# Three groups' sums in one pair of PSUM banks, and the variance floor made once per twelve tiles

## The chip, the cores and the metric

The kernel runs on one core of a Trainium2 chip. The metric is the device time of one execution in microseconds. Five engines work side by side, each through its own instructions in order: PE (matmuls; its weight loads have rows of their own, PEld), DVE, ACT, POOL and SP, which here only issues DMAs. They wait for each other through semaphores.

## The reference

Two stages follow each other: attention through 32 inducing points (each batch's tokens are pooled into 32 vectors, then each token attends to these), and a feed-forward layer whose activation is `h * softmax(h)` with a layer norm over the 1,024 hidden values. Cut to what matters (`e` is the exponential, `c` the token's row):

```python
h = mab(I, x)                 # per batch: 32 pooled vectors from 12608 tokens
y = mab(x, h)                 # each token attends to the 32 vectors
hid = y @ w_in                # 128 -> 1024
e = exp(hid - max(hid))
solu = hid * e / (sum(e) + 1e-9)
ln = (solu - mean(solu)) / sqrt(var(solu) + 1e-6) * g_ln
out = ln @ w_out              # 1024 -> 128
```

There are 4 batches of 12,608 tokens and 128 features, all in float32.

## The kernel before, in words

A tile is 128 tokens; a batch has 99 tiles (the last one half full), the four batches 396. Tiles go in groups of four (the last group of a batch has three), 25 groups a batch. Three groups make a set (`FG = 3`): eight full sets and one set of a single group per batch, 36 sets in all.

A batch's first pass (`p1`: loading x, transposing it, pooling) runs among the previous batch's tiles, except for batch 0, whose first pass runs alone at the start. `p2` makes the attention weights of twelve tiles at a time. Then each tile goes through `main`, `soft` and `products`:

- PE makes the 1,024 hidden values of the tile (L958) in a PSUM buffer of two banks; DVE multiplies by the token's factor and takes the negated maximum (L996);
- ACT takes the exponential and sums it into S, one column per tile (L1006);
- POOL multiplies by the hidden values (L1010), which takes 2.37 us and is the longest step of a tile;
- ACT squares the product and sums it into Q (L1021); DVE transposes it in 32x32 blocks into the group's `vt` (L1034);
- when a group's four tiles are in `vt`, its product with the weights `wc` starts (`products`, L1079). It runs in two streams, w = 0 and 1, of 32 steps each. A stream owns two of the four 32-row groups of the PE array and two PSUM banks, `op0` or `op1`. A step of one stream, which I call a beat, is two matmuls. Where both streams are open their beats go side by side; the hidden values (L958) and the transposes (L551) also use only half of the array and are paired with a beat of one stream. Where nothing is paired with it, a beat has the array to itself.

The matmul has 129 columns: 128 outputs and the sum over the hidden values, from a column of ones. When a stream's 32 beats are done, `evacuate` copies its two banks (2 x 129 columns) to the set's buffer `raw` (L1101), on DVE or ACT, whichever the planner finds first. The lock `OP[w]` has one buffer: the stream's next group starts when the copy is done.

The layer norm is finished once per set, since the division by the sum of exponentials cancels against the variance up to the floor 1e-6, which becomes (1e-3 S)^2. `floor` (per group) makes this on POOL in two small instructions (L1051, L1052), writes it beside Q, and deals Q and the floor through DRAM into the token order of the products (one DMA out, L1055, and one in per tile, L1063). `finish` (per set) makes the variance, its inverse root and a Newton step on POOL and ACT (L1122 to L1141), and then scales the set's outputs group by group, either as four ACT instructions (L1156) or as one POOL instruction (L1152). `stored` writes them out.

The order of every engine is settled at build time by `Planner`. Each step is an `Op` with an engine, an estimated cost, the steps it follows, a priority (the tile's number plus an offset), and perhaps an alternative engine (`alt`). The planner always takes the engine that could start something first, and of what is ready there the step with the lowest priority. So a changed cost or a step on another engine can move all steps behind it, on every engine.

```python
pick = min(
    (o for o in self.ops if o[0].eng == eng and o[1] <= limit),
    key=lambda o: (o[2][1] if o[0].prio is None else o[0].prio, o[3]),
)
```

Of the kernel before, what the change touches and what calls it, by code (L numbers as in the profile page):

```python
# [8 lines left out]
F32 = mybir.dt.float32  # L9
# [237 lines left out]
def set_attention_then_solu_kernel(ctx: ExitStack, tc: tile.TileContext, x, inducing, w_in, w_out, g_ln, out):  # L247
# [38 lines left out]
    def small(i, **widths):  # L286
# [20 lines left out]
    OP = [Lock(), Lock()]  # L307
    HN, EU = Lock(hn_b[:1]), Lock()
# [9 lines left out]
        dict(qe=buf([P, GS, 2], f"qe{i}"), S=buf([P, GS], f"st{i}"), dd=dd_pool.tile([P * 2 * GS], F32, name=f"dd{i}")) for i in range(4)  # L318
# [3 lines left out]
        dict(dl=buf([P, 4 * FG, 2], f"dl{i}"), **dict(zip(("part", "v", "y", "root", "z"), split(buf([P, 5, 4 * FG], f"fin{i}")))))  # L322
# [588 lines left out]
    fin = {(b, f): dict(buf=Event(), out=[], left=2 * min(FG, NG - f * FG)) for b in range(NB) for f in range(-(-NG // FG))}  # L911
# [74 lines left out]
    def soft(t, hp, d):  # L986
# [14 lines left out]
        if not A["left"]:  # L1001
# [4 lines left out]
            "ACT", 1133, lambda: nc.scalar.activation(e, hn, AF.Exp, bias=nm, scale=-1.0, accum_out=G["S"][:, s : s + 1]), d, rel, srel,  # L1006
# [39 lines left out]
    def floor(b, j):  # L1046
        G = grp[(b, j)]
        n = ff_groups[j][1]
        ep = G["qe"][:, :n, 1]
        gt, gs = nc.gpsimd.tensor_tensor, nc.gpsimd.tensor_scalar  # L1050
        d = yield Op("POOL", 165, lambda: gs(out=ep, in0=G["S"][:, :n], scalar1=1e-3, scalar2=1e-12, op0=ALU.mult, op1=ALU.add), G["squared"])  # L1051
        d = yield Op("POOL", 125, lambda: gt(out=ep, in0=ep, in1=ep, op=ALU.mult), d)  # L1052
        flat = G["dd"][: P * 2 * n].rearrange("(p f) -> p f", f=2 * n)
        ds = yield dma(
            P * 8 * n, lambda: nc.sync.dma_start(flat, G["qe"][:, :n, :].rearrange("p s v -> p (s v)")), d, G["squared"], prio=-30, issue=600  # L1055
        )
        F = fin[(b, j // FG)]
        rel = yield F["buf"]
        dl = F["dl"][:, j % FG * 4 : j % FG * 4 + 4, :]
        laid = G["dd"][: P * 2 * n].rearrange("(a t s v) -> s t a v", a=4, t=M, v=2)  # L1060
        dealt = []
        for s in range(n):
            d = yield dma(P * 8, lambda: nc.sync.dma_start(dl[s * M : (s + 1) * M], laid[s]), ds, rel, prio=-30, issue=600)  # L1063
            dealt.append(d)
        plan.set(G["floor"], *dealt)
        give(ST, G["stb"], *dealt)

    def products(b, j, t, w):
# [4 lines left out]
        op, rel = yield OP[w]  # L1073
# [3 lines left out]
        def emit(a, k):  # L1077
            q = slice(a * M, (a + 1) * M)
            nc.tensor.matmul(op[:rows, a - 2 * w, : C + 1], lhsT=vt[q, k, :], rhs=wc[q, k, :], start=(k == 0), stop=(k == JB - 1))  # L1079
# [13 lines left out]
    def evacuate(b, j, w, op, dop, prio):  # L1093
# [3 lines left out]
        i0 = j % FG * 4 + 2 * w  # L1097
        rel = yield F["buf"]

        def copied(eng):  # L1100
            return lambda: eng(F["raw"][:rows, i0 : i0 + 2, :], op[:rows, :, : C + 1])  # L1101

        d = yield Op("DVE", 340, copied(nc.vector.tensor_copy), dop, rel, prio=prio, alt=Op("ACT", 265, copied(nc.scalar.copy), dop, rel, prio=prio))
# [6 lines left out]
    def finish(b, f):  # L1110
# [8 lines left out]
        part, v, y, root, z = (F[k][:rows, :w] for k in ("part", "v", "y", "root", "z"))  # L1119
        Q, ep = (F["dl"][:rows, :w, i] for i in range(2))  # L1120
        gt, gs = nc.gpsimd.tensor_tensor, nc.gpsimd.tensor_scalar
        d = yield Op("ACT", 110, lambda: nc.scalar.activation(part, F["raw"][:rows, :w, C], AF.Square, scale=1.0 / FF), F["out"])  # L1122
# [153 lines left out]
```

## Time and profile before

| | us |
|---|---|
| median of 3 runs (1237.88 to 1242.12) | 1241.6 |
| the profiled execution, its own time | 1239.79 |
| its span | 1238.0 |
| mean granted clock of PE | 0.984 |

The profile is of one execution. A row of a group of instructions has the line, engine, operation, output and inputs, shapes and count; behind the bar the busy time, the mean length of one in ns, and the idle time ahead of them with what ended it. A row of the waits has who waited for whom, the total in us, how often, and the longest. A timeline row begins with start and length in us. Matmul counts are twice those of the program, since a float32 matmul shows as two.

### The profile page before, as it was taken

What the parts mean: (1) busy time and instruction counts of PE and PEld (TensorE: products, weight loads), DVE (VectorE), ACT (ScalarE), POOL (GpSimd) and SP (SyncE); (2) the same over time, 40 slices, a digit from 0 to 9 for tenths busy, and PEclk for the clock granted to TensorE, in tenths of its full rate; (3) what the DMA queues carried; (4) which work ended last, traced back from release to release, by engine and by line L of the source; (5) the groups of instructions that cost most, each with busy time, mean ns of one, the idle gap of its engine ahead of it and who ended that gap; (6) DMA issues with size and microseconds to landing.
All of it is one profiled execution on the core that took longest, in us unless ns stands there. A gap on an engine that the chain in (4) does not pass through costs nothing. (4 is left out here: it accounts for less than half of the span.)

```text
span 1238.0 us, 79230 instructions
## 1 busy us (share of the span) xinstructions
PE 1199.9 (97%) x35686; PEld 1113.8 (90%) x35686; DVE 1126.6 (91%) x1822; ACT 1126.7 (91%) x2408; POOL 1100.6 (89%) x984
## 2 busy tenths in 40 slices
PE   9889999999999999999999999999999999999995
PEld 6688899999899999999999998989999999999995
DVE  5669999999998999989999999999999999999982
ACT  5569999999899999999999999999989999999993
POOL 2569889889998999989999999998989999999994
PEclk9869999999999999999999999999999999999998
DMA  9462334322233333233133224432122222211111
GB/s 355 177 155 64 120 110 131 107 68 79 56 89 114 113 99 113 85 107 91 47 93 120 62 73 133 124 122 70 43 81 58 58 56 56 56 48 38 30 31 42
DMA packets 134867, 113.69 MB, mean 92 GB/s; under 512 B 79072, under 2 KB 87168, under 8 KB 134400
## 3 DMA queue, kind: packets, MB, share of 16 engines
q1 hardware_dynamic: 134528, 108.63, 29.6%
q8 instruction: 279, 4.57, 1.5%
q14 instruction: 60, 0.49, 0.1%
HBM read 54.30 MB, written 52.18 MB: 86 GB/s over the span
## 5 line engine op out<-in xcount | busy, mean ns | idle before, releaser
L1079 PE MATMUL op<-wc,vt 32*128 32x129 f32 x25600 | 1020.0, 274 | 8.2 <-DVE vt L1034 1.9
L1079 PEld LDWEIGHTS op<-wc,vt 32*128 32x128 f32 x25600 | 976.5, 185 | 47.3 <-issue 32.1
L1010 POOL TENSOR_TENSOR eu<-spare,eu 128x1024 f32<-128x1024 f32 x192 | 454.0, 2372 | 33.0 <-ACT eu L1006 30.1
L958 PE MATMUL h<-hs,aT 32*128 32x128 f32 x6336 | 431.3, 277 | 7.1 <-DVE spare L996 3.1
L1034 DVE STREAM_TRANSPOSE vt<-eu 128x1024 f32<-128x1024 f32 x330 | 404.0, 1231 | 6.9 <-POOL eu L1010 6.9
L958 PEld LDWEIGHTS h<-hs,aT 32*128 32x128 f32 x6336 | 388.5, 189 | 21.8 <-DVE spare L996 6.8
L1021 ACT ACTIVATE sq<-eu 128x1024 bf16<-128x1024 f32 x330 | 346.9, 1051 | 34.2 <-POOL eu L1010 29.8
L1010 POOL TENSOR_TENSOR eu<-hn,eu 128x1024 f32<-128x1024 f32 x138 | 326.8, 2374 | 21.6 <-ACT eu L1006 19.5
L996 DVE TENSOR_SCALAR_CACHE_REDUCE spare<-h,rn 128x1024 f32<-128x1024 f32 x228 | 286.5, 1263 | 22.3 <-PE h L958 10.9
L996 DVE TENSOR_SCALAR_CACHE_REDUCE hn<-h,rn 128x1024 f32<-128x1024 f32 x168 | 211.0, 1263 | 13.9 <-PE h L958 5.6
L1006 ACT ACTIVATE eu<-spare,nm 128x1024 f32<-128x1024 f32 x192 | 218.9, 1141 | 4.2 <-DVE spare L996 3.6
L1006 ACT ACTIVATE eu<-hn,nm 128x1024 f32<-128x1024 f32 x138 | 157.3, 1141 | 0.1
L1156 ACT ACTIVATE os<-spare,fin 128x128 f32<-128x128 f32 (+1 forms) x276 | 86.4, 389 | 2.9 <-DMA out_dram<-os 1.8
L1010 POOL TENSOR_TENSOR spare<-spare 128x1024 f32<-128x1024 f32 x36 | 85.4, 2373 | 0.8 <-ACT spare L1006 0.7
L1034 DVE STREAM_TRANSPOSE vt<-spare 128x1024 f32<-128x1024 f32 x66 | 81.3, 1232 | 2.3 <-POOL spare L1010 2.0
L1021 ACT ACTIVATE sq<-spare 128x1024 bf16<-128x1024 f32 x66 | 69.4, 1052 | 5.8 <-POOL spare L1010 4.8
L1010 POOL TENSOR_TENSOR spare<-hn,spare 128x1024 f32<-128x1024 f32 x30 | 71.2, 2373 | 2.9 <-ACT spare L1006 2.8
L1101 DVE COPY spare<-op 128x258 f32<-128x258 f32 (+1 forms) x123 | 50.8, 417 | 20.0 <-PE op L1079 18.4
L1021 ACT ACTIVATION_READ_ACCUMULATOR sq<-eu 128x1 f32 x330 | 62.7, 190 | 0.0
L551 PE MATMUL h<-ident,xn 32*128 32x32 f32 x1188 | 45.5, 220 | 0.4 <-issue 0.4
L551 PEld LDWEIGHTS h<-ident,xn 32*128 32x128 f32 x1188 | 44.1, 137 | 1.2 <-ACT spare L1101 0.6
L608 ACT COPY xT<-h 128x768 f32<-128x768 f32 (+2 forms) x54 | 39.6, 733 | 2.9 <-PE h L551 2.8
(166 smaller groups left out, 1026.0 us busy)
## 6 DMA issues: line engine op xcount, KB each, us to landing
xT<-xd SPq DMA_DIRECT2D x96, 256.0 KB, 3.3
out_dram<-os SPq DMA_DIRECT2D x96, 256.0 KB, 2.3
xn<-in_x_dram SPq DMA_DIRECT2D x73, 256.0 KB, 3.2
xd<-xT SPq DMA_DIRECT2D x72, 256.0 KB, 2.5
dl<-dd SPq DMA_DIRECT2D x396, 1.0 KB, 2.7
xd<-vt SPq DMA_DIRECT2D x7, 768.0 KB, 11.0
spare<-in_x_dram SPq DMA_DIRECT2D x5, 768.0 KB, 12.8
wc<-hn SPq DMA_DIRECT2D x16, 128.0 KB, 2.7
```

Of the source, the lines that this page charges most:

```text
L551: nc.tensor.transpose(out=tr[:h, at : at + M], in_=block[rows, :h], identity=ident[rows, rows])
L608: nc.scalar.copy(in_rows(xT[:, :n, :], c0), from_rows(tr, n))
L958: nc.tensor.matmul(hp[:, cols], lhsT=aT[rows, i // 2, :], rhs=hs[rows, cols], start=True, stop=True)
L996: lambda: nc.vector.tensor_scalar(out=hn, in0=hp, scalar1=rn, scalar2=None, op0=ALU.mult, op1=ALU.min, accum_out=nm),
L1006: "ACT", 1133, lambda: nc.scalar.activation(e, hn, AF.Exp, bias=nm, scale=-1.0, accum_out=G["S"][:, s : s + 1]), d, rel, srel,
L1010: d = yield Op("POOL", 2330, lambda: nc.gpsimd.tensor_tensor(out=e, in0=hn, in1=e, op=ALU.mult), de, prio=t + PR_MU)
L1021: "ACT", 1040, lambda: nc.scalar.activation(sq, e, AF.Square, scale=1.0 / 32.0, accum_out=G["qe"][:, s, 0:1]), d,
L1034: lambda: nc.vector.transpose(out=G["vtb"][:, : n * FF].rearrange("p (j s t) -> p j s t", j=M, s=n)[:, :, s, :], in_=e.rearrange("p (a f) ...
L1079: nc.tensor.matmul(op[:rows, a - 2 * w, : C + 1], lhsT=vt[q, k, :], rhs=wc[q, k, :], start=(k == 0), stop=(k == JB - 1))
L1101: return lambda: eng(F["raw"][:rows, i0 : i0 + 2, :], op[:rows, :, : C + 1])
L1156: nc.scalar.activation(os[:rows, q, :], raw[:, q, :], AF.Copy, scale=y[:, i0 + q : i0 + q + 1])
```

## The change

The sums of a set's three groups go side by side into the same two banks of a stream: group i of the set writes columns 129 i to 129 (i + 1). A new lock `TURN[w]` lets a stream take the groups in order; it is given on when a group's last beat is planned, without a copy between. Only the set's first group takes `OP[w]`, and only its last starts `evacuate`, which copies all columns at once (2 x 387 of them, or 2 x 129 for the single group at a batch's end). The planner's costs for the copy become 90 + 269 k on DVE and 90 + 215 k on ACT for k groups.

The floor's two POOL instructions go. ACT sums the exponentials straight into the buffer that is dealt, beside Q, so S and Q are dealt; `finish` makes the floor for the whole set with one ACT Square, with scale 1e-3 and bias 1e-12, after the dealt data have landed.

```diff
+    TURN = [Lock([None]), Lock([None])]
...
-        dict(qe=buf([P, GS, 2], f"qe{i}"), S=buf([P, GS], f"st{i}"), dd=...) for i in range(4)
+        dict(qe=buf([P, GS, 2], f"qe{i}"), dd=...) for i in range(4)
...
-            "ACT", 1133, lambda: nc.scalar.activation(e, hn, AF.Exp, ..., accum_out=G["S"][:, s : s + 1]), d, rel, srel,
+            "ACT", 1133, lambda: nc.scalar.activation(e, hn, AF.Exp, ..., accum_out=G["qe"][:, s, 1:2]), d, rel, srel,
...
     def floor(b, j):
-        ep = G["qe"][:, :n, 1]
-        d = yield Op("POOL", 165, lambda: gs(out=ep, in0=G["S"][:, :n], scalar1=1e-3, scalar2=1e-12, ...), G["squared"])
-        d = yield Op("POOL", 125, lambda: gt(out=ep, in0=ep, in1=ep, op=ALU.mult), d)
...
-            ..., lambda: nc.sync.dma_start(flat, G["qe"]...), d, G["squared"], prio=-30, issue=600
+            ..., lambda: nc.sync.dma_start(flat, G["qe"]...), G["squared"], prio=-30, issue=600
...
     def products(b, j, t, w):
-        op, rel = yield OP[w]
+        F, i = fin[(b, j // FG)], j % FG
+        yield TURN[w].at(b * NG + j)
+        rel = ()
+        if not i:
+            F["op"][w], rel = yield OP[w]
+        op = F["op"][w]
...
-            nc.tensor.matmul(op[:rows, a - 2 * w, : C + 1], ...)
+            nc.tensor.matmul(op[:rows, a - 2 * w, i * (C + 1) : (i + 1) * (C + 1)], ...)
...
-            spawn(evacuate(b, j, w, op, d, t + PR_EV), t + PR_EV)
+            F["todo"][w] -= 1
+            if not F["todo"][w]:
+                spawn(evacuate(b, j, w, op, d, t + PR_EV), t + PR_EV)
+            give(TURN[w], None)
...
     def evacuate(b, j, w, op, dop, prio):
-        d = yield Op("DVE", 340, copied(nc.vector.tensor_copy), ..., alt=Op("ACT", 265, ...))
+        d = yield Op("DVE", 90 + 269 * k, copied(nc.vector.tensor_copy), ..., alt=Op("ACT", 90 + 215 * k, ...))
...
     def finish(b, f):
+        fd = yield Op("ACT", 210, lambda: nc.scalar.activation(ep, S, AF.Square, scale=1e-3, bias=tiny[:rows]), fd)
```

Three places show how the order moves. The first is PE in batch 1, where stream 1 (`op1`) comes to the end of its fourth group, in the middle of a set, and goes on with the fifth; `xn1` rows are the first pass's transposes. Before:

```order
L1079 MATMUL op0_665<-wc_157,vt_65 128x129 x2
L1079 MATMUL op1_666<-wc_157,vt_65 128x129 x2
L1079 MATMUL op0_665<-wc_157,vt_65 128x129 x10
L958 MATMUL h1_664<-hs1_125,aT0_94 128x128 x2
L1079 MATMUL op0_665<-wc_157,vt_65 128x129 x2
L958 MATMUL h1_664<-hs1_125,aT0_94 128x128 x2
L1079 MATMUL op0_665<-wc_157,vt_65 128x129 x2
L958 MATMUL h1_664<-hs1_125,aT0_94 128x128 x2
L1079 MATMUL op0_665<-wc_157,vt_65 128x129 x2
L958 MATMUL h1_664<-hs1_125,aT0_94 128x128 x2
L1079 MATMUL op0_665<-wc_157,vt_65 128x129 x2
L551 MATMUL h0_663<-ident_138,xn1_68 128x32 x6
```

And now, at the same two groups (lines are 2 higher there):

```order
L959 MATMUL h1_660<-hs1_121,aT0_94 128x128 x2
L1081 MATMUL op1_662<-wc_153,vt_65 128x129 x2
L1081 MATMUL op0_661<-wc_153,vt_65 128x129 x2
L1081 MATMUL op1_662<-wc_153,vt_65 128x129 x2
L1081 MATMUL op0_661<-wc_153,vt_65 128x129 x2
L1081 MATMUL op1_662<-wc_153,vt_65 128x129 x2
L1081 MATMUL op0_661<-wc_153,vt_65 128x129 x2
L1081 MATMUL op1_662<-wc_153,vt_65 128x129 x2
```

Before, stream 1 is off behind the second row: stream 0 runs five beats (x10) with nothing beside them and then four beside hidden values, until stream 1's next group starts beside the last row; now the old group's last beat and the new group's first stand one behind the other.

The second place is PE at the end of the set that holds these groups, where both streams close. Now:

```order
L1081 MATMUL op0_661<-wc_153,vt_65 128x129 x2
L1081 MATMUL op1_662<-wc_153,vt_65 128x129 x4
L959 MATMUL h0_659<-hs1_121,aT0_94 128x128 x8
L1081 MATMUL op0_661<-wc_153,vt_65 128x129 x2
L959 MATMUL h1_660<-hs1_121,aT1_96 128x128 x8
L1081 MATMUL op1_662<-wc_153,vt_65 128x129 x2
```

Both streams end within one beat of each other; ahead of stream 0's first beat of the next set stand four beats of hidden values with nothing beside them, and ahead of stream 1's first beat four more, one beside stream 0.

The third place is POOL in batch 3, in `finish` of the set whose inverse roots are made behind the 366th product (the 364th in the changed order). Before:

```order
L1138 TENSOR_TENSOR fin1_117<-fin1_117 128x12
L1139 TENSOR_TENSOR fin1_117<-fin1_117 128x12
L1140 TENSOR_SCALAR fin1_117<-fin1_117 128x12
L1141 TENSOR_TENSOR fin1_117<-fin1_117 128x12
L1051 TENSOR_SCALAR qe3_111<-st3_112 128x4
L1152 TENSOR_TENSOR os0_100<-spare_66,fin1_117 128x512
L1052 TENSOR_TENSOR qe3_111<-qe3_111 128x4
L1010 TENSOR_TENSOR spare_66<-spare_66 128x1024
```

And now on POOL:

```order
L1150 TENSOR_TENSOR fin1_113<-fin1_113 128x12
L1151 TENSOR_TENSOR fin1_113<-fin1_113 128x12
L1152 TENSOR_SCALAR fin1_113<-fin1_113 128x12
L1153 TENSOR_TENSOR fin1_113<-fin1_113 128x12
L1011 TENSOR_TENSOR eu_84<-spare_66,eu_84 128x1024 x2
```

with ACT at the same set:

```order
L1145 ACTIVATE fin1_113<-fin1_113 128x12
L1022 ACTIVATE sq_83,qe3_108<-eu_84 128x1024
L1007 ACTIVATE eu_84,qe0_102<-spare_66,nm1_115 128x1024
L1022 ACTIVATE sq_83,qe3_108<-eu_84 128x1024
L882 ACTIVATE nr1_92<-nr1_92 128x8
L1168 ACTIVATE os1_101<-spare_66,fin1_113 128x128 x4
L1168 ACTIVATE os0_100<-spare_66,fin1_113 128x128 x4
L1007 ACTIVATE spare_66,qe0_102<-spare_66,nm2_116 128x1024
```

The floor's two steps are gone from POOL, and the group that POOL scaled is scaled on ACT. Over the whole program the scaling stands on POOL 31 times before and 11 times now, on ACT 69 and 89 times; the copies out of the banks are 123 on DVE and 77 on ACT before, 40 and 32 now.

More of the change, by code (lines that the diff above doesn't have):

```diff
@@ L317, in set_attention_then_solu_kernel @@
     ST = Lock([
-        dict(qe=buf([P, GS, 2], f"qe{i}"), S=buf([P, GS], f"st{i}"), dd=dd_pool.tile([P * 2 * GS], F32, name=f"dd{i}")) for i in range(4)
+        dict(qe=buf([P, GS, 2], f"qe{i}"), dd=dd_pool.tile([P * 2 * GS], F32, name=f"dd{i}")) for i in range(4)
     ])
@@ L910, in set_attention_then_solu_kernel @@
     part_of = {(b, s): (k, s - s0) for b in range(NB) for k, (s0, n) in enumerate(at_groups[b]) for s in range(s0, s0 + n)}
-    fin = {(b, f): dict(buf=Event(), out=[], left=2 * min(FG, NG - f * FG)) for b in range(NB) for f in range(-(-NG // FG))}
+    fin = {(b, f): dict(buf=Event(), out=[], left=2, op=[None] * 2, todo=[min(FG, NG - f * FG)] * 2) for b in range(NB) for f in range(-(-NG // FG))}
     grp = {(b, j): dict(vt=Event(), st=Event(), floor=Event(), turned=[], squared=[], over=[]) for b in range(NB) for j in range(NG)}
@@ L1005, in soft @@
         de = yield Op(
-            "ACT", 1133, lambda: nc.scalar.activation(e, hn, AF.Exp, bias=nm, scale=-1.0, accum_out=G["S"][:, s : s + 1]), d, rel, srel,
+            "ACT", 1133, lambda: nc.scalar.activation(e, hn, AF.Exp, bias=nm, scale=-1.0, accum_out=G["qe"][:, s, 1:2]), d, rel, srel,
             prio=t + PR_EX,
@@ L1096, in evacuate @@
         rows = ff_groups[j][1] * M
-        i0 = j % FG * 4 + 2 * w
+        k = j % FG + 1
         rel = yield F["buf"]
         def copied(eng):
-            return lambda: eng(F["raw"][:rows, i0 : i0 + 2, :], op[:rows, :, : C + 1])
-        d = yield Op("DVE", 340, copied(nc.vector.tensor_copy), dop, rel, prio=prio, alt=Op("ACT", 265, copied(nc.scalar.copy), dop, rel, prio=prio))
+            return lambda: eng(
+                F["raw"][:rows, : 4 * k, :].rearrange("p (j a) c -> p j a c", a=4)[:, :, 2 * w : 2 * w + 2].rearrange("p j a c -> p a j c"),
+                op[:rows, :, : k * (C + 1)].rearrange("p a (j c) -> p a j c", c=C + 1),
+            )
+        d = yield Op(
+            "DVE", 90 + 269 * k, copied(nc.vector.tensor_copy), dop, rel, prio=prio,
+            alt=Op("ACT", 90 + 215 * k, copied(nc.scalar.copy), dop, rel, prio=prio),
+        )
         give(OP[w], op, d)
@@ L1118, in finish @@
             fd += d
-        part, v, y, root, z = (F[k][:rows, :w] for k in ("part", "v", "y", "root", "z"))
-        Q, ep = (F["dl"][:rows, :w, i] for i in range(2))
+        part, ep, v, y, root, z = (F[k][:rows, :w] for k in ("part", "ep", "v", "y", "root", "z"))
+        Q, S = (F["dl"][:rows, :w, i] for i in range(2))
         gt, gs = nc.gpsimd.tensor_tensor, nc.gpsimd.tensor_scalar
+        fd = yield Op("ACT", 210, lambda: nc.scalar.activation(ep, S, AF.Square, scale=1e-3, bias=tiny[:rows]), fd)
         d = yield Op("ACT", 110, lambda: nc.scalar.activation(part, F["raw"][:rows, :w, C], AF.Square, scale=1.0 / FF), F["out"])
```

8 lines of the change are left out of this document (3 added, 5 removed).

## The prediction

> **What bounds the kernel now.** I read the shares of the page first, then its chain of work that ended last, and then the busy time of each engine by stretches.
>
> ```profile
> PE 1199.9 (97%) x35686; PEld 1113.8 (90%) x35686; DVE 1126.6 (91%) x1822; ACT 1126.7 (91%) x2408; POOL 1100.6 (89%) x984
> ...
> PE 18%; POOL 14%; issue 3%; ACT 2%; DMA 1%; POOLq 0%; SPq 0%; DVE 0%; ACTq 0%
> ```
>
> PE is busy 97% of the span and its weight loads, DVE, ACT and POOL 89 to 91%, so relief of one engine alone buys little. The chain names PE and POOL. The stretches show where each of them leads (columns: stretch, length, then PE, PEld, DVE, ACT, POOL busy us with counts, granted clock, DMA share, GB/s).
>
> ```profile
> 100.00:1000.00 900.00, 890.43 (x27418) 827.56 (x27418) 856.00 (x1384) 850.37 (x1804) 831.70 (x736) 1.00 0.31 90
> 700.00:800.00 100.00, 98.68 (x3162) 92.11 (x3158) 96.52 (x157) 97.28 (x204) 98.15 (x87) 1.00 0.37 108
> 1000.00:1180.00 180.00, 176.85 (x5576) 171.22 (x5573) 173.51 (x242) 178.05 (x387) 177.48 (x155) 1.00 0.18 47
> ```
>
> There are two stages. From 100 to 1000 us (the batches that share the engines with the next batch's first pass) PE is busy 98.9% and ACT 850.4 us of 900, or 94.5%; of the nine hundreds of us in it ACT's fullest, the second row, has 97.3%. From 1000 to 1180 us ACT is busy 178.05 of 180 (98.9%) and POOL 177.5 (98.6%). The clock is granted in full throughout.
>
> **PE: fewer half-empty beats.** A beat is one k-step of a pair of row groups. What a beat costs, full and half empty, stands in the timeline and in the chain.
>
> ```profile
> 1200.92 7.43 PE L1079 MATMUL op<-wc,vt 32*128 32x129 f32 x256 [0.68 <-ACT spare L1101]
> ...
> 963.20 0.89 PE h L958 x16
> ```
>
> A whole group on both streams takes 7.43 us, 0.232 us for each of its 32 double beats; four beats of one pair alone take 0.89, so a half-empty beat costs as much as a full one. I count program order: before has 4,447 beats, 584 of them half empty; after has 4,349 with 375. That is 98 beats less, 98 x 0.232 = 22.7 us. The lists show why: inside a twelve-tile set a stream goes on with the next group in the next beat, where nine beats of the others lay between before. What it does at a set's end is a rival below.
>
> **POOL: the floor goes, and most of the scaling.**
>
> ```profile
> L1052 POOL TENSOR_TENSOR qe<-qe 128x4 f32<-128x4 f32 x96 | 19.7, 205 | 1.6
> L1051 POOL TENSOR_SCALAR qe<-st 128x4 f32<-128x4 f32 x96 | 19.0, 198 | 0.0
> ...
> L1152 POOL TENSOR_TENSOR os<-spare,fin 128x512 f32<-128x512 f32 x28 | 29.0, 1040 | 0.8 <-DMA out_dram<-os 0.8
> ```
>
> The floor's 200 instructions go: 38.7 us in these rows and 1.6 for the eight narrow ones, 40.3. The planner's order also changes sides: the scaling of outputs stands on POOL 11 times instead of 31, 20 x 1.04 = 20.8 us less. POOL loses 61 us.
>
> **ACT: the scaling arrives, and the new Square.**
>
> ```profile
> L1156 ACT ACTIVATE os<-spare,fin 128x128 f32<-128x128 f32 x272 | 85.1, 389 | 2.9 <-DMA out_dram<-os 1.8 <-POOL fin L1141 1.1
> ...
> L1101 ACT COPY spare<-op 128x258 f32<-128x258 f32 x73 | 26.1, 362 | 6.0 <-PE op L1079 5.5
> ...
> L608 ACT COPY xT<-h 128x768 f32<-128x768 f32 x42 | 33.0, 786 | 2.5 <-PE h L551 2.5
> ...
> L1122 ACT ACTIVATE fin<-spare 128x12 f32<-128x12 f32 x32 | 6.9, 216 | 0.5 <-DVE spare L1101 0.2
> ...
> L708 ACT ACTIVATE small<-m,small 128x1 f32<-128x1 f32 x32 | 9.2, 288 | 8.6 <-DVE small L700 8.5
> ```
>
> 272 scalings are 68 groups of four, 85.1 / 68 = 1.25 us a group; 20 more groups are +25.0 us. The Square of the floor over 12 columns is not in the trace: by L1122 it is 0.216, by L708 (with a bias from memory) 0.288, so 36 are 7.8 to 10.4; I take 7.8, the same shape. Copies out of PSUM: 31 wide and 1 narrow one instead of 77. 774 columns in two banks are not in the trace: one old copy (0.36) bounds them below, three (1.09) above, and L608, 0.786 for 768 columns of PSUM, is the nearest row. With 0.79 they take 24.9 us where the old ones took 27.5 (26.1 in the row, 1.4 for four narrow ones): -2.6. ACT gains **+30 us**.
>
> **DVE.**
>
> ```profile
> L1101 DVE COPY spare<-op 128x258 f32<-128x258 f32 x119 | 49.1, 416 | 12.3 <-PE op L1079 10.8
> ...
> L996 DVE TENSOR_SCALAR_CACHE_REDUCE spare<-h,rn 128x1024 f32<-128x1024 f32 x228 | 286.5, 1263 | 22.3 <-PE h L958 10.9 <-ACT eu L1006 5.8 <-issue 1.8
> ```
>
> Between these two readers of PSUM a column costs (1263 - 416) / 766 = 1.1 ns, so 774 columns take about 0.99 us (0.79, ACT's row, and 1.25, three old copies, bound it). 33 of these and 7 narrow ones are 35.6 us against 50.8 (49.1 in the row, 1.7 for four narrow ones): -15 us.
>
> **Waits that move.**
>
> ```profile
> ACT sq L1021 <- POOL eu L1010: 29.8, 40, 2.5
> ...
> POOL fin L1125 <- DMA dl<-dd: 6.2, 1, 6.2
> ...
> PEld op L1079 <- ACT spare L1101: 4.4, 12, 0.9
> PEld op L1079 <- DVE spare L1101: 4.3, 9, 0.7
> ...
> SPq L1055 <- POOL qe L1052: 216.1, 73, 5.3
> ```
>
> SP's queue no longer stands for POOL before it stores S and Q; it stands for ACT's squares, which it waits for already, so the deals land earlier and the loads queued behind them are not later: 0 us. In exchange the new Square makes ACT wait for the dealt data, with exponentials and squares queued behind it. POOL had that wait (L1125) and was held by it once, in the tail; I take 0, and each wait that does appear costs its length. ACT's 29.8 us of standing for POOL should shrink, POOL being lighter.
>
> **The sum.** With PE 22.7 us, POOL 61 and DVE 15 lighter and ACT 30 heavier, **ACT becomes the bound**. Of the 20 scaling groups 16 fall before tile 300 of 396 (the three batches of stage one are 297 tiles), with 27 of the Squares (5.8 us), and the copies there cost the same (51 x 0.36 against 23 x 0.79): +25.8. So stage one asks 876.2 us of ACT. Filled to 97.3% (its fullest stretch there) it lasts 900.5, no gain; filled to 98.9%, as in the last stage, 885.9, a gain of 14.1. POOL's relief speaks for the second, the first pass still sharing the engines for the first. I take the middle, 98.1%: 893.2, **-6.8 us**. PE fits: it saves more than that.
>
> In the last stage POOL's work ended late; the tail shows it.
>
> ```profile
> 1208.75 1.17 ACT L1006 ACTIVATE eu<-spare,nm 128x1024 f32<-128x1024 f32 x1
> ...
> 1213.40 2.35 POOL L1010 TENSOR_TENSOR eu<-spare,eu 128x1024 f32<-128x1024 f32 x1
> ...
> 1215.78 1.25 DVE L1034 STREAM_TRANSPOSE vt<-eu 128x1024 f32<-128x1024 f32 x1 [1.23 <-POOL eu L1010]
> ...
> 1217.75 0.43 DVE L1101 COPY spare<-op 128x258 f32<-128x258 f32 x1 [0.72 <-PE op L1079]
> ...
> 1218.23 7.34 PE L1079 MATMUL op<-wc,vt 32*96 32x129 f32 x256 [0.52 <-DVE spare L1101]
> ```
>
> ACT's last exponential ends at 1209.9, POOL takes up its product only at 1213.4: 3.5 us of backlog. POOL loses about 10 us there (25 floors at 0.4), while ACT gains 4 x 1.25 + 9 x 0.216 - 2.3 (9 copies of 0.79 for 26 of 0.36) = 4.6 at 98.9% busy. The exponential then ends 4.6 later and its product starts at once: +1.1. The last group's matmuls wait for the copy ahead of them, now 0.99 for 0.43: +0.6. Together -6.8 + 1.7 = -5.1. The profiled execution took 1239.8 us (1238.0 of span and 1.8 around it), 0.15% under the median of 1241.6, so I forecast **1234.7**, 0.6% under the median. A measurement of this kernel can tell about 0.5% from no change: 1235.4 to 1247.8 is "the same".
>
> **Rivals.**
>
> *PE leads to the end.* ACT merely fills its idle time (49.6 us of it in stage one) and the 22.7 us of beats come through: 1217. For it: PE is 99% busy there and leads the chain. Against: 876 us in 877 would be 99.9% of ACT. With ACT at 98.9% in stage one, still in this case, 1227.
>
> *Nothing comes of it.* The half-empty beats were time in which PE waited for tiles anyway, and ACT at 97.3% makes the same pace: 1240.
>
> *Slower: ACT can't be filled.* The scalings stand in ACT's order ahead of exponentials, so POOL and DVE wait behind them, and ACT stays at 96%, between its average and its best: 876.2 / 0.96 = 912.7, +12.7, and in the last stage +4.6 with no backlog to absorb it and +0.6: 1258. It turns slower than before below 97.3%. For it: ACT's average of 94.5%; against: the idle time was mostly waiting for POOL.
>
> *Slower: both streams stop at a set's end.* Three groups fill the same banks and both streams end within a few beats, so PE has only the next tile's first product until the copies are done. The gap of 0.52 us at 1218.23 with its copy of 0.43 becomes 1.08. Over 36 sets that is 39 us uncovered, +16 net of the beats: 1256; with four lone beats (0.89) ahead of each restart, as the order has it at the place shown, 7 us, which ACT's bound hides. The order was read at one such place only. It decides from 22.7 / 36 = 0.63 us of standing per set.
> The Trainium skill's page "Perfetto Trace Analysis", section "Optimizing Tensor Performance", "Matmuls", speaks for this rival: independent groups of matmuls should go through different banks in turn, so that one is copied out under the next one's matmuls. By that rule the time would be 1256; the trace of before has only 4.4 + 4.3 us in which weight loads stood for a copy with one bank a group and stream, so I give it little.
>
> **How the numbers follow.** Forecast, 1230 to 1239: 0.40, a little over half of it under 1235.4. PE leads: 0.18. Nothing: 0.18. ACT not filled: 0.16. Sets' ends: 0.08, all slower. Faster 0.24 + 0.18 = 0.42; same 0.16 + 0.18 = 0.34; slower 0.24. The range, 1217 to 1252, leaves out the worse part of both slower cases and what lies under the second.
>
> **What would show it.** Right: ACT at 97.5 to 99% from 100 to 1000 us, its busy time near 1157, POOL's near 1040; L1079's beats with few lone ones; wide copies near 0.99 on DVE and 0.79 on ACT. Wrong: weight loads standing for the copies by more than 20 us, ACT standing for dealt data, or ACT's share in stage one unchanged (slower) while PE stays full (then PE leads).

## The result, and the profile after

| | before | after |
|---|---|---|
| median, us | 1240.49 (1237.88 to 1242.12, 4 runs) | 1226.43 (1224.25 to 1227.57, 4 runs) |
| span of the profiled execution, us | 1238.0 | 1225.3 |

The ratio is 0.9889, with a 95% interval of 0.9871 to 0.9908: 14 us faster. The forecast had 7. The profile's page and the stretches of the changed kernel, in the columns used before, with the hundred from 700 us and the last stage:

```profile
PE 1180.9 (96%) x35679; PEld 1091.4 (89%) x35679; DVE 1114.9 (91%) x1745; ACT 1151.3 (94%) x2479; POOL 1051.5 (86%) x758
...
PE 56%; ACT 21%; DVE 8%; issue 7%; POOL 4%; DMA 2%; SPq 1%; POOLq 0%; ACTq 0%; DVEq 0%
...
100.00:1000.00 900.00, 886.44 (x27862) 821.14 (x27864) 858.86 (x1340) 884.21 (x1902) 806.82 (x573) 1.00 0.32 91
700.00:800.00 100.00, 98.68 (x3124) 90.22 (x3128) 95.14 (x158) 99.15 (x212) 90.73 (x64) 1.00 0.39 118
1000.00:1180.00 180.00, 172.60 (x5496) 165.52 (x5490) 168.84 (x224) 177.75 (x381) 167.15 (x112) 0.99 0.16 44
```

ACT is now the fullest engine but PE: 884.2 of 900 us, 98.2%, where it had 94.5%. POOL has gone from 92.4% to 89.6%. The chain follows PE and ACT.

Fixed stretches hold different work in the two kernels. So I cut both at the same two places, the inverse roots of the first set of batch 0 and of the last set of batch 2, about 3 batches apart; the second row goes on to the end. Before:

```profile
121.30:973.20 851.90, 842.99 (x26017) 782.50 (x26009) 809.98 (x1313) 804.17 (x1713) 784.96 (x698) 1.00 0.32 93
973.20:1238.00 264.80, 247.68 (x7759) 239.94 (x7753) 228.74 (x314) 241.96 (x527) 244.73 (x224) 0.98 0.17 44
```

And after:

```profile
121.80:961.40 839.60, 826.65 (x25970) 764.00 (x25966) 800.57 (x1256) 824.53 (x1780) 749.73 (x534) 1.00 0.32 94
961.40:1225.30 263.90, 246.97 (x7840) 238.11 (x7834) 227.47 (x297) 246.22 (x532) 232.42 (x171) 0.97 0.16 44
```

The same work takes 851.9 us and 839.6: 12.3 of the 12.7 us that the span loses lie in the first stage, 0.9 in the rest (and half a microsecond is lost at the start). In the first stage ACT does 20.4 us more in 12.3 us less. What it no longer does is wait. ACT's waits for others between 100 and 1000 us, the longest rows (who waited for whom, us in total, times, longest), before:

```profile
ACT sq L1021 <- POOL eu L1010: 23.8, 33, 1.8
ACT spare L1101 <- PE op L1079: 4.3, 8, 0.9
ACT sq L1021 <- POOL spare L1010: 3.5, 7, 1.0
```

And after:

```profile
ACT aT L898 <- PE h L552: 4.2, 7, 1.0
ACT spare L1106 <- DVE spare L1106: 1.6, 3, 0.7
ACT small L709 <- DVE small L701: 1.3, 2, 1.0
ACT sq L1022 <- POOL eu L1011: 1.0, 3, 0.5
```

All of ACT's waits in the stage together fall from 42.6 us to 11.6, and 26 of these 31 are its squares (`sq`) standing for POOL's products. The other side of it is in the waits of the whole execution: POOL's products in `eu` now stand for ACT's exponentials 72.9 us where they stood 49.6.

The groups that the forecast put a length on (line, engine, operation, shapes, count, busy us, mean ns, idle ahead):

```profile
L1168 ACT ACTIVATE os<-spare,fin 128x128 f32<-128x128 f32 x344 | 106.7, 389 | 2.2 <-POOL fin L1153 1.2 <-DMA out_dram<-os 0.8
...
L1106 DVE COPY spare<-op 128x774 f32<-128x774 f32 x33 | 31.6, 958 | 6.9 <-ACT spare L1106 4.7 <-PE op L1081 1.5
...
L1106 ACT COPY spare<-op 128x774 f32<-128x774 f32 x31 | 24.8, 801 | 4.2 <-DVE spare L1106 2.5 <-PE op L1081 1.3 <-DVE small L694 0.2
...
L1133 ACT ACTIVATE fin<-dl,tiny 128x12 f32<-128x12 f32 x32 | 9.7, 304 | 1.5 <-DMA dl<-dd 1.4
```

### The profile page after: what moved, and what is told of

It reads as the page before. It is cut to its first block, busy times and chain, and to the rows that moved or that the text cites. A ratio compares the mean times of both kernels' runs of the same rounds, so it can differ in the third digit from the quotient of the medians.

```text
span 1225.3 us, 79047 instructions
## 1 busy us (share of the span) xinstructions
PE 1180.9 (96%) x35679; PEld 1091.4 (89%) x35679; DVE 1114.9 (91%) x1745; ACT 1151.3 (94%) x2479; POOL 1051.5 (86%) x758
## 3 DMA queue, kind: packets, MB, share of 16 engines
q1 hardware_dynamic: 134528, 108.63, 29.8%
## 4 chain that ended last, share of the span: by engine, by line
PE 56%; ACT 21%; DVE 8%; issue 7%; POOL 4%; DMA 2%; SPq 1%; POOLq 0%; ACTq 0%; DVEq 0%
PE op L1081 36%; PE h L959 11%; ACT sq L1022 9%; ACT eu L1007 5%; DVE spare L997 3%; ACT os L1168 2%; POOL eu L1011 2%; DVE vt L1035 2%; PE h L552 2%; ACT spare L1007 1%; PE h L742 1%; PE h L660 1%; PE h L857 1%; DVE spare L1106 1%; DVE hn L997 1%
## 5 line engine op out<-in xcount | busy, mean ns | idle before, releaser
L1081 PE MATMUL op<-wc,vt 32*128 32x129 f32 x25600 | 1000.4, 275 | 11.4 <-ACT spare L1106 4.3
L1081 PEld LDWEIGHTS op<-wc,vt 32*128 32x128 f32 x25600 | 958.2, 186 | 49.3 <-issue 33.0
L959 PE MATMUL h<-hs,aT 32*128 32x128 f32 x6336 | 438.0, 279 | 10.7 <-DVE spare L997 5.7
L959 PEld LDWEIGHTS h<-hs,aT 32*128 32x128 f32 x6336 | 393.7, 191 | 31.2 <-DVE spare L997 9.6
L1168 ACT ACTIVATE os<-spare,fin 128x128 f32<-128x128 f32 x356 | 110.5, 389 | 2.2 <-POOL fin L1153 1.2
L1106 DVE COPY spare<-op 128x774 f32<-128x774 f32 (+1 forms) x40 | 34.6, 865 | 15.1 <-PE op L1081 9.5
L1007 ACT ACTIVATE spare<-spare,nm 128x1024 f32<-128x1024 f32 x36 | 41.1, 1141 | 0.0
```

Source lines behind the costliest of these rows:

```text
L959: nc.tensor.matmul(hp[:, cols], lhsT=aT[rows, i // 2, :], rhs=hs[rows, cols], start=True, stop=True)
L1081: nc.tensor.matmul(op[:rows, a - 2 * w, i * (C + 1) : (i + 1) * (C + 1)], lhsT=vt[q, k, :], rhs=wc[q, k, :], start=(k == 0), stop=(k == JB ...
L1106: return lambda: eng(F["raw"][:rows, : 4 * k, :].rearrange("p (j a) c -> p j a c", a=4)[:, :, 2 * w : 2 * w + 2].rearrange("p j a c -> p a ...
L1168: nc.scalar.activation(os[:rows, q, :], raw[:, q, :], AF.Copy, scale=y[:, i0 + q : i0 + q + 1])
```

## The experiments

The forecast's theory, A: ACT is the bound, and what is taken off the others counts only until ACT is full. Its rivals: TensorE bounds (C); no engine does, and the order in which the planner sets the work through all of them makes the time (B). Ratios are to the kernel before on the same chip, with their 95% intervals; 1% is 12.4 us. All numbers on engines are from one profiled execution each.

### Each half of the change alone, planned anew

`banks_only` is the change without the floor's part: shared banks and wide copies, the floor on POOL as before.

```diff
--- after
+++ banks_only
+        d = yield Op("POOL", 165, lambda: gs(out=ep, in0=G["S"][:, :n], scalar1=1e-3, scalar2=1e-12, ...), G["squared"])
+        d = yield Op("POOL", 125, lambda: gt(out=ep, in0=ep, in1=ep, op=ALU.mult), d)
...
-        fd = yield Op("ACT", 210, lambda: nc.scalar.activation(ep, S, AF.Square, scale=1e-3, ...), fd)
```

> The changed banks and the single copy per set, with the floor on POOL as before. Its order has 4,358 beats on PE, 400 of them half empty (before 4,448 and 585, changed kernel 4,350 and 376); scaling on ACT for 73 groups. If the gain is the banks' (streams that need not stop, fewer beats): 1226 to 1231 us, ACT about 97 to 98% busy from 100 to 1000 us. If the gain is the floor's (a lighter POOL that lets ACT fill): 1237 to 1241. If it takes both: about 1233.

Measured: 0.9938 (0.9915 to 0.9961), 1236.72 us: by the ratio 7.7 us faster, about half of the change, as expected "if it takes both". ACT is at 94.7% between 100 and 1000 us, as before the change, so this gain isn't one of a fuller ACT.

`floor_only` is the other half: banks and copies as before, the floor as in the change.

```diff
--- before
+++ floor_only
-        d = yield Op("POOL", 165, lambda: gs(out=ep, in0=G["S"][:, :n], ...), G["squared"])
-        d = yield Op("POOL", 125, lambda: gt(out=ep, in0=ep, in1=ep, op=ALU.mult), d)
...
+        fd = yield Op("ACT", 210, lambda: nc.scalar.activation(ep, S, AF.Square, scale=1e-3, ...), fd)
```

> Only the floor moved (S and Q dealt, one ACT Square per set), with one copy per group and the banks as before. Its order has 4,481 beats, 654 half empty, so more than before; POOL is 40 us lighter; scaling on ACT for 81 groups. If the gain is the banks': 1238 to 1246, no faster than before. If it is the floor's: 1226 to 1231. If it takes both: about 1233.

Measured: 1.0015 (0.9999 to 1.0031), as expected if the gain is the banks'. ACT is at 95.6%. Moving the floor gains nothing by itself in this one order. What it adds to the banks (0.9938 to 0.9889) is no larger than what the next runs show that another order does.

### The same work in another order

Four kernels differ from before or after only in the planner's estimate of the copy, by 5 or 10 ns; the instructions are the same, their order is another, and with it which engine gets a copy or a scaling group.

```diff
--- before
+++ before_jitter (345, 270), before_order2 (350, 275)
-        d = yield Op("DVE", 340, ..., alt=Op("ACT", 265, ...))
+        d = yield Op("DVE", 345, ..., alt=Op("ACT", 270, ...))
--- after
+++ after_jitter (95), after_order2 (100)
-            "DVE", 90 + 269 * k, ..., alt=Op("ACT", 90 + 215 * k, ...)
+            "DVE", 95 + 269 * k, ..., alt=Op("ACT", 95 + 215 * k, ...)
```

> The kernel before with the same instructions; only the planner's estimate of the copy is 5 ns longer (345 and 270), which changes the order: 4,473 beats, 636 half empty. If the order alone moves the time as much as the change did, this differs from before by 8 us or more in either direction. If the change's gain is one of work and waits, it stays within 5 us of 1240.5.

> The changed kernel with the same instructions but for the side of some scalings; only the planner's estimate of the copy is 5 ns longer, which changes the order: 4,331 beats, 342 half empty, scaling on ACT for 83 groups. If the gain is one of work and waits: 1221 to 1231, and the 6 groups fewer on ACT (7 us) may show. If the measured order was a lucky draw: 1232 to 1240.

> The changed kernel with the copy's estimate 10 ns longer on both engines in the planner (100 in place of 90 ns of fixed cost), which only makes another order of the same work (22 beats fewer). Theory R, the change gives about 1% by rule and the order scatters by some 0.4%: ratio 0.987 to 0.996. Theory L, luck of one order: 0.996 or more.

> The kernel before with the copy's estimate 10 ns longer on both engines in the planner (350 and 275), another order of the same work, with 26 beats fewer and 8 scaling groups more on ACT. Theory R: ratio 0.997 to 1.006. Theory L: an order of before as good as that of the change exists nearby, ratio under 0.995.

| | beats | half empty | ratio | ACT, 100 to 1000 us |
|---|---|---|---|---|
| before | 4,447 | 584 | 1 | 94.5% |
| before_jitter | 4,473 | 636 | 1.0036 (1.0020 to 1.0053) | 94.0% |
| before_order2 | 4,421 | 540 | 1.0064 (1.0049 to 1.0079) | 94.4% |
| after | 4,349 | 375 | 0.9889 (0.9871 to 0.9908) | 98.2% |
| after_jitter | 4,331 | 342 | 0.9938 (0.9914 to 0.9963) | 96.1% |
| after_order2 | 4,328 | 341 | 0.9953 (0.9930 to 0.9975) | 96.6% |

The beats are counted by pairing neighbours in the program order; no view of the profile holds these counts, and another way of pairing gives others (the expectations above have one more for before and after). Four things are to be read here. Another order, with the sides that it gives to copies and scalings, is worth 0.4 to 0.6%, half of what the change is worth. The sides alone don't explain it: both new orders of before scale more groups on ACT (73 and 78 instead of 69) and both of after fewer (83 and 84 instead of 89), and all four are slower. By the expectations this is luck in part: before_jitter's 4.5 us (by the ratio) fit a gain of work and waits, but after_jitter's 1235.7 us lie in the range given to a lucky draw, after_order2 lies at the upper end of theory R, and before_order2 a little above R's range. But each order of after beats each of before, and the means (0.9927 against 1.0033) are 1.1% apart, so with three orders each the change itself gives about 1%. And within one kernel the beats don't say which order is good: before_order2 has the fewest of its three and is the slowest, and both new orders of after have fewer beats than after and are slower. ACT at 98.2% belongs to one order too, as the two stretches show (after_jitter, then after_order2): the same work fills ACT only to 96.1 and 96.6%. (These two are from executions of 1241.1 and 1239.8 us, near the slow end of what these kernels take.)

```profile
100.00:1000.00 900.00, 877.87 (x27382) 811.01 (x27376) 841.63 (x1317) 864.66 (x1845) 794.09 (x565) 1.00 0.32 90
...
100.00:1000.00 900.00, 883.89 (x27454) 817.06 (x27450) 847.98 (x1324) 869.00 (x1857) 799.14 (x568) 0.99 0.32 91
```

### What a microsecond more costs on each engine

Four kernels are after, in its own order, with an instruction or two added to one engine whose result nothing uses, once for each of the 100 groups of four tiles: a copy of 64 columns on ACT, an instruction of 4 columns on POOL, one of 128 columns on DVE, two transposes on PE.

```diff
--- after
+++ after_act_pad
-            "ACT", 1133, lambda: nc.scalar.activation(e, hn, AF.Exp, ...), d, rel, srel,
+            "ACT", 1133, lambda: (nc.scalar.activation(e, hn, AF.Exp, ...), nc.scalar.activation(pad[:, 1, :64], pad[:, 0, :64], AF.Copy) if not s else None), d, rel, srel,
+++ after_pool_pad, behind POOL's product
+... nc.gpsimd.tensor_scalar(out=pad[:, 1, :4], in0=pad[:, 0, :4], scalar1=1e-3, scalar2=1e-12, ...) if not s ...
+++ after_dve_pad, behind DVE's transpose
+... nc.vector.tensor_scalar(out=pad[:, 1, :], in0=pad[:, 0, :], scalar1=1e-3, scalar2=1e-12, ...) if not s ...
+++ after_pe_pad, ahead of the hidden values, whose buffer it writes
+                for _ in range(0 if s else 2):
+                    nc.tensor.transpose(out=hp[:, :P], in_=ident, identity=ident)
```

> The changed kernel with one small copy more on ACT for each group of four (about 100, some 0.2 us each, about 20 us of ACT; every other instruction and the order stay). Theory A, ACT is the bound of the stage (98.2% busy there): nearly all of the 20 us shows, ratio to the kernel before about 1.003 to 1.005, ACT still 98% in 100 to 1000 us. Theory B, the order's chain through several engines sets the rate and no engine alone: about half shows, ratio 0.995 to 0.999. Theory C, TensorE is the bound: under 5 us shows, ratio 0.989 to 0.993.

> The changed kernel with one small arithmetic instruction more on POOL for each group of four (about 100, some 0.2 us each, about 20 us of POOL). POOL has 11% of room in 100 to 1000 us. Theory A (ACT bounds): under 5 us shows, ratio 0.989 to 0.993. Theory B (a chain through POOL): about half shows, 0.995 to 0.999. Theory C (TensorE): as A.

> The changed kernel with one small arithmetic instruction more on DVE for each group of four (about 100, some 0.15 to 0.2 us each, 15 to 20 us of DVE). DVE has 4.6% of room in 100 to 1000 us. Theory A (ACT bounds): under 5 us shows, ratio 0.989 to 0.993. Theory B (a chain through several engines): about half shows, 0.994 to 0.998. Theory C (TensorE): as A.

> The changed kernel with two transposes of 128 columns more on TensorE for each group of four (about 200, some 0.06 to 0.1 us each, 12 to 20 us of TensorE; their output is written over). Theory C (TensorE, 98.5% busy, is the bound): all of it shows, ratio 0.999 to 1.005. Theory B: about half, 0.994 to 0.998. Theory A (ACT bounds and TensorE's rows are only stretched by its waits): under 5 us, 0.989 to 0.993.

The time added is the ratio less after's 0.9889, times 1241 us; the busy time is that of the page less after's.

| pad on | ratio | time added, us | engine's busy time added, us | share that shows |
|---|---|---|---|---|
| ACT | 0.9950 (0.9933 to 0.9968) | 7.6 | 12.8 | 0.59 |
| POOL | 0.9937 (0.9916 to 0.9958) | 6.0 | 14.4 | 0.42 |
| PE | 1.0166 (1.0149 to 1.0184) | 34 | 42.8 | 0.80 |
| DVE | 1.0549 (1.0513 to 1.0586) | 82 | 97.9 | 0.84 |

The intervals of ACT and POOL are some 3 us wide to each side, so their shares are rough. But no theory with one bound stands: if ACT alone were it, its share would be near 1 and POOL's near 0; were it PE, ACT's would be near 0. Theory B's "about half" fits ACT and POOL. The pads on PE and DVE turned out far larger than meant. The transpose's rows are 0.30 us, and each takes 128 rows, where a beat of one stream takes 64; DVE's pad mostly stands for POOL (last section), so its 0.84 is the price of holding DVE up and not of work on DVE. A large load may also cost more of itself than a small one, since it comes nearer to being the bound; that wasn't tried.

### The edits in the old order

If the beats and POOL's work have a price, it must show where they are taken away and nothing else moves. Five kernels keep the order of before, the planner's costs included, and change only what is sent to an engine. before_pe_less leaves out 98 half-empty beats and before_full_less 98 full ones, spread over the program; before_floor_gone sends no floor; before_scale_swap sends 20 of POOL's 31 scaling groups to ACT at the same place; before_all_terms has the first, the third and the fourth of these edits.

```diff
--- before
+++ before_pe_less
+            go = [p for w in pairs for p in (stream[w],) if p["j"] < JB and p["ready"] <= plan.now + i * BEAT + EAGER]
+            if len(go) == 1 and not also and 0 < go[0]["j"] < JB - 1:
+                lone[0] += 1
+                gone = lone[0] * 98 // LONE != (lone[0] - 1) * 98 // LONE
...
+                if not gone:
                     p["emit"](2 * w, p["j"])
                     p["emit"](2 * w + 1, p["j"])
+++ before_full_less
+            if len(go) == 2 and not also and all(0 < p["j"] < JB - 1 for p in go):
+++ before_floor_gone
+... accum_out=G["qe"][:, s, 1:2] ...
+        d = yield Op("POOL", 165, lambda: None, G["squared"])
+        d = yield Op("POOL", 125, lambda: None, d)
+++ before_scale_swap
             def scaled():
+                pools[0] += 1
+                if pools[0] * 20 // 31 != (pools[0] - 1) * 20 // 31:
+                    return scaled_act()
```

> The kernel before, in its own order, without 98 of its half-empty beats (those 98 steps of the second product are left out; 22.7 us of TensorE at 0.232 us). It asks what the beats alone are worth. Theory P, TensorE is the bound and its price is that of the pad (about 0.78 us per us): -17.7 us, ratio about 0.986. Theory A, of the forecast, ACT stands right behind and stops the gain: about -6.8 us, ratio about 0.9945, and ACT then at 98% in 100 to 1000 us.

> The kernel before, in its own order, without 98 of its full beats (98 steps of the second product of both streams are left out; 22.7 us of TensorE). Theory F, half-empty beats only fill the wait for the other stream's block, full ones are real work: a gain, -8 to -18 us, ratio 0.986 to 0.994. Theory S, TensorE has slack in the order of before whatever the beat: as without the half-empty ones, ratio 0.998 to 1.002.

> The kernel before, in its own order, without the 200 small floor instructions on POOL (40.3 us; the raw sums are dealt and used in the floor's place). Theory P, POOL has a price of about 0.3 as by its pad: -12 us, ratio about 0.990. Theory A, POOL is not on the path in the first stage and only the last stage gains: 0 to -4 us, ratio 0.997 to 1.000.

> The kernel before, in its own order, with 20 of the 31 scaling groups that POOL does done on ACT at the same places (ACT +23 us at 1.17 us a group, POOL -20.8 us). Theory P (ACT's price 0.3 to 0.6, POOL's 0.3): +1 to +8 us, ratio 1.001 to 1.006. Theory A (ACT at 94.5% fills up to 98% first): 0 to +5 us in the first stage plus up to 5 us in the last, ratio 1.000 to 1.008; this run alone doesn't part the two, it gives the term for the sum.

> The three edits together in the order of before: 98 beats gone, floor gone, 20 scaling groups on ACT; no wide copies, no new order. Theory P: the sum of the three, -22 to -29 us, ratio 0.977 to 0.982, more than the change itself (0.9889), whose new order then costs the rest. Theory A (ACT bound once the beats are gone): as the change, ratio 0.988 to 0.992 with ACT at 98% in 100 to 1000 us.

| | ratio | time, us | engine's busy time, us (by rows) |
|---|---|---|---|
| before_pe_less | 1.0010 (0.9994 to 1.0026) | +1 | PE -1.7 (-22.7) |
| before_full_less | 0.9969 (0.9957 to 0.9982) | -4 | PE -7.8 (-22.7) |
| before_floor_gone | 0.9975 (0.9960 to 0.9991) | -3 | POOL -30.6 (-40.3) |
| before_scale_swap | 1.0117 (1.0077 to 1.0156) | +14.5 | ACT +22.3 (+25.0), POOL -18.3 (-20.8) |
| before_all_terms | 1.0087 (1.0064 to 1.0111) | +11 | PE -4.3, ACT +21.5, POOL -49.8 |

Only before_floor_gone falls into a range that was expected (theory A's); before_full_less lies between its two, and the other three fit neither theory. Left out in the old order, the half-empty beats are worth nothing, full ones a sixth of their length, and POOL's 30 us give 3. The work moved to ACT costs about two thirds of itself (0.4 to 0.9 by the interval). All three edits together are 11 us slower than before, where the change is 14 us faster. So some 25 us lie in what these edits don't have: the shared banks with their fewer copies, and the plan made anew with them. These runs don't part the two.

Why the half-empty beats are worth nothing is seen where one was left out. The timeline rows of PE around one run of beats (start and length in us; matmul records of a group behind x), before:

```profile
503.68 2.44 PE L1079 MATMUL op<-wc,vt 32*128 32x129 f32 x66
505.94 0.28 PE L958 MATMUL h<-hs,aT 32*128 32x128 f32 x2
```

And in before_pe_less, the same place 2.2 us later:

```profile
505.87 2.46 PE L1086 MATMUL op<-wc,vt 32*128 32x129 f32 x62
508.14 0.28 PE L965 MATMUL h<-hs,aT 32*128 32x128 f32 x2
```

One beat (four records) less, and from the start of the run to the next hidden value it takes 2.27 us instead of 2.26. In the starts of the single records, the matmuls of stream 1 begin 0.82 us after the run's start before and 0.83 without the beat: they wait for DVE's copy out of their bank, which isn't faster. Its rows, before and without the beat:

```profile
504.06 0.39 DVE L1101 COPY spare<-op 128x258 f32<-128x258 f32 x1
...
506.26 0.39 DVE L1108 COPY spare<-op 128x258 f32<-128x258 f32 x1
```

By the single records both copies end 0.055 us before stream 1's first matmul. So at this place stream 0's beat only lay in a wait for the bank; for the other 97 it is not shown. Busy time doesn't show it: the records of these matmuls are 0.27 us long and normally start 0.11 us apart, so the 0.22 us between two starts that the missing beat leaves are still covered.

And the wait taken away in one place comes back in another. The waits of the whole execution for the copies of the sums (DVE and ACT standing for PE's products) and for the squares, before_floor_gone:

```profile
DVE spare L1101 <- PE op L1079: 25.3, 33, 7.4
...
ACT sq L1021 <- POOL eu L1010: 19.7, 28, 2.5
ACT spare L1101 <- PE op L1079: 17.6, 16, 7.2
```

Before, these were 18.4, 29.8 and 12.7. With the floor gone ACT stands 10 us less for POOL, and DVE and ACT stand 12 us more for sums that they are to copy, which holds what is queued behind.

`before_scale_act` asks whether a new plan does better than the old order with more work on ACT.

```diff
--- before
+++ before_scale_act
-            done = yield Op("ACT", 1170, scaled_act, dy, rel, alt=Op("POOL", 1000, scaled, dy, rel))
+            done = yield Op("ACT", 1170, scaled_act, dy, rel)
```

> The kernel before with all scaling on ACT (the 31 groups that POOL does go to ACT: +36 us of ACT at 1.17 us a group, -32 us of POOL), planned anew. If a plan can't absorb it (as the 20 groups in the old order): 31/20 of 1.2%, ratio about 1.018. If the plan absorbs most of it: 0.998 to 1.007.

Measured: 1.0084 (1.0065 to 1.0103), between the two expectations. 31 groups cost 10.4 us when planned, where 20 cost 14.5 unplanned (9.5 to 19): about half the price for each, but not free.

### The copies

`after_split` makes each wide copy as three narrow ones at the same place.

```diff
--- after
+++ after_split
-            return lambda: eng(F["raw"][:rows, : 4 * k, :]..., op[:rows, :, : k * (C + 1)]...)
+            def three():
+                for i in range(k):
+                    eng(F["raw"][:rows, 4 * i + 2 * w : 4 * i + 2 * w + 2, :], op[:rows, :, i * (C + 1) : (i + 1) * (C + 1)])
```

> The changed kernel in its own order with each wide copy of 774 columns made as three of 258 at the same place (rows: DVE 33 times 3 x 0.417 - 0.958 = +9.7 us, ACT 31 times 3 x 0.361 - 0.801 = +8.7 us). If the length of the copies carries the gain: half or more of it shows, ratio 0.994 to 0.998. If the new order carries it: 0 to 4 us, ratio 0.989 to 0.992.

Measured: 0.9883 (0.9868 to 0.9897), the same as after. DVE's busy time is 4.0 us longer and ACT's 3.0, not 9.7 and 8.7. That a wide copy is shorter than three narrow ones carries nothing that the measurement (some 3 us to each side) can tell.

`after_narrow` keeps the shared banks and copies each group's sums as soon as the group is done.

```diff
--- after
+++ after_narrow
-            if not F["todo"][w]:
-                spawn(evacuate(b, j, w, op, d, t + PR_EV), t + PR_EV)
+            spawn(evacuate(b, j, w, op, d, t + PR_EV, not F["todo"][w]), t + PR_EV)
...
+        d = yield Op("DVE", 340, copied(nc.vector.tensor_copy), ..., alt=Op("ACT", 265, ...))
+        if last:
+            give(OP[w], op, *F["cp"][w])
```

> The changed kernel with the shared banks, but each group's sums copied out by itself when the group is done (200 narrow copies as before, planned anew; the bank is given back after the third; 4,344 beats). Theory B, the streams that go on without a wait for their bank carry the gain: ratio 0.987 to 0.995. Theory C, fewer copies for DVE and ACT carry it: 0.997 or more.

Measured: 1.0207 (1.0191 to 1.0223). By the number this is in theory C's range (0.997 or more), but it is slower than before too, and its waits show another reason:

```profile
PEld op L1081 <- DVE spare L1105: 29.3, 54, 0.8
...
PE op L1081 <- DVE spare L1105: 17.8, 46, 0.6
PEld op L1081 <- ACT spare L1105: 14.6, 25, 1.4
...
PE op L1081 <- ACT spare L1105: 8.7, 21, 1.2
```

The next group's matmuls write beside columns that are still to be copied, and they got a wait for that copy, of which the planner knows nothing. Weight loads stand 43.9 us for copies, against 10.0 in after. (The matmuls' rows are not added: each of their waits lies inside one of the weight loads'.) So this run doesn't part the two theories. It shows what it costs when the streams stop between groups unplanned: 1268.58 us, by the ratios some 39 more than after.

## Why the prediction was half right

**Right.** The direction, the stage, and the engine that fills: ACT at 98.2% from 100 to 1000 us (forecast 98.1), the gain there and hardly any behind it. The wide copies take 0.958 and 0.801 us (0.99 and 0.79). The dealt data cost next to nothing: the Square's wait for them is 1.4 us. ACT's standing for POOL's products in `eu` shrank, as the text expected, from 29.8 to 3.8 us over the whole execution.

**The step that failed** is the sum for the first stage, "876.2 us of ACT ... 893.2, -6.8 us": the stage gained 12.3. Between the two cuts above the stage asked 20.4 us more of ACT, where the forecast's +25.8 comes to 24.4 (851.9 of 900 us of the stage). 804.2 + 20.4 at 98.2% are the 839.6 us measured; with 24.4 it would have been 843.8, 4 us more. The rows themselves came out as forecast. ACT's scaling and the new Squares between the cuts, one row of before and two of after:

```profile
L1156 ACT ACTIVATE os<-spare,fin 128x128 f32<-128x128 f32 x188 | 58.8, 389 | 0.0
...
L1168 ACT ACTIVATE os<-spare,fin 128x128 f32<-128x128 f32 x252 | 78.2, 389 | 1.0 <-DMA out_dram<-os 0.8
...
L1133 ACT ACTIVATE fin<-dl,tiny 128x12 f32<-128x12 f32 x23 | 7.0, 306 | 0.0
```

With the narrow ones the scaling is 20.6 us more, the Squares 7.8, the copies 1.5 less: +26.9 by rows, where the engine's busy time grew by 20.4. So the term was mis-sized because it adds the busy times of rows one by one, and rows of one engine overlap their neighbours. In before_scale_swap it is the same (25.0 by rows, 22.3 busy), on the whole of ACT (+30 forecast, +24.6 busy), and on POOL (61 by rows, 49 busy). The rest of the difference, a little over 1 us, is the share (98.2% instead of 98.1) and where the stretch is cut. The last stage was put at +1.7 and gave -0.9.

**As a cause, the step holds only in part.** "ACT becomes the bound" makes the sum come out for the one order that was measured, but a pad on ACT shows 0.59 of itself, pads on PE, DVE and POOL show too, and two other orders of the same work, at 96.1 and 96.6%, take 1235.7 and 1236.7 us. The forecast took 98.1% from a band of 97.3 to 98.9 as if the work decided it; the order does, so the 98.2% measured is in part luck, and so is it that 1234.7 lies close to those two.

**"98 x 0.232 = 22.7 us" for PE** was priced wrong. The beat does last 0.232 us in the rows, but leaving 98 half-empty ones out of the old order gives nothing, and 98 full ones 4 us. The rival "PE leads" rested on this price and falls with it. That fewer beats are worth more in a plan made with them is not excluded. The rival "nothing comes of it" had a reason for the beats that fits (they lay in a wait, at the one place shown) and the wrong end, since the change did more than take beats away.

**The slower rivals.** "ACT can't be filled" came half true in two orders, below the 97.3% at which it was to turn slower, and they were faster than before all the same: the demand on which that threshold rests was too high. "Both streams stop at a set's end": weight loads stand 10.0 us for copies after (6.3 + 3.7) and 8.7 before (4.4 + 4.3), 1.3 us more where the rival put 39. The rows of after:

```profile
PEld op L1081 <- ACT spare L1106: 6.3, 9, 2.2
...
PEld op L1081 <- DVE spare L1106: 3.7, 9, 0.7
```

The rule of the Trainium skill that spoke for it (page "Perfetto Trace Analysis", section "Optimizing Tensor Performance", "Matmuls": go through the banks in turn) isn't borne out by this kernel: banks_only, whose groups of a set go into one pair of banks, is 0.6% faster, and its weight loads stand for copies as long as before (8.7 us). That the other stream and the tiles' first products fill the time of the copy fits the order shown at the one place, but no run was made to show it.

**What was shown, and what stays open.** Shown: the gain is about 1% over three orders of each kernel; most of it comes with the shared banks when planned anew (0.6% in the one order of banks_only that was run, 0.9% against the mean of the three of before); it is not the length of the copies, and it isn't had by taking beats, the floor or POOL's scaling out of the old order. Open: whether the shared banks help because a stream goes on without its copy, with more beats side by side, or because DVE and ACT have 72 copies to place among their other work instead of 200. The waits of DVE and ACT ahead of these copies seem to speak for the second. Before, then after:

```profile
DVE spare L1101 <- PE op L1079: 18.4, 27, 7.4
ACT spare L1101 <- PE op L1079: 12.7, 11, 7.2
...
DVE spare L1106 <- PE op L1081: 9.5, 8, 7.0
...
DVE spare L1106 <- ACT spare L1106: 4.7, 6, 1.6
...
ACT spare L1106 <- DVE spare L1106: 2.5, 5, 0.7
...
ACT spare L1106 <- PE op L1081: 1.3, 2, 0.8
```

Waits for a finished product fall from 31.1 us to 10.8, but the wide copies also stand for each other, so it is 18.0 us in all, and in after_jitter and after_order2 26.8 and 27.0, as in before_order2 (26.9). So these waits belong to the order, and no run parts the two explanations. No kernel tried is faster than after by more than the measurement tells.

## What to carry to other kernels

In this kernel, whose engines are all busy nine tenths of the time and whose order is laid down in advance, taking work from one engine in the old order gained almost nothing (0 to 0.17 us per microsecond), while adding some cost 0.4 to 0.8 of it. In such a kernel a sum of row lengths against one bound is a poor forecast. What paid here was a dependency fewer with the order laid anew; and before such a gain is believed, the order should be shaken by a few nanoseconds of an estimate, since that alone moved this kernel by 0.4 to 0.6%. Price an instruction by the time from its start to the start of the next one and not by its row's length, and price work that only fills a wait at nothing until a run without it says otherwise.

## What the runs showed of the hardware

A small instruction on DVE stood for POOL's. The pad of after_dve_pad, a scaling of 128 columns from SBUF to SBUF, takes 0.18 us in the median of the 15 that began with no POOL product running, and 1.24 us in the mean of the other 85. Each of those ends 0.08 to 0.14 us behind the end of that product. Rows of the timeline (start, length), the first on POOL, the other two on DVE:

```profile
503.07 7.01 POOL L1013 TENSOR_TENSOR eu<-spare,eu 128x1024 f32<-128x1024 f32 x3 [0.16 <-ACT eu L1009]
...
505.53 2.31 DVE L1040 TENSOR_SCALAR pad<-pad 128x128 f32<-128x128 f32 x1
507.76 1.23 DVE L1037 STREAM_TRANSPOSE vt<-eu 128x1024 f32<-128x1024 f32 x1
```

The second of POOL's three products ends at 507.75, the scaling at 507.84. The Trainium skill, page "SBUF — State Buffer", section "Who interferes with whom", says that a `tensor_scalar` of DVE in a mode with two ports takes the pair of ports that it shares with GpSimd as a whole, and whichever comes second is blocked until the other is done; the wait in this trace agrees, though the trace doesn't name the mode. The transposes beside it run at 1.23 us under POOL's products and don't wait.

On ACT, rows overlap: in after_act_pad 100 copies of 0.243 us, 24.3 us by rows, made ACT 12.8 us busier.
